# A ratio moved eight steps behind the sums it is made from, and a unit's sums, inverse, scaling and turn moved one to three steps later

## The chip, the core and the metric

The kernel runs on one core of a Trainium2 chip. A core has a matrix engine (PE in the profile, with its weight loads as PEld), a vector engine (DVE, called VectorE below), a scalar engine (ACT, ScalarE), a general engine (POOL, GpSimd), and SyncE (SP), which issues most of the DMAs. Each engine works through its own list of instructions in order; an instruction whose input is not there yet holds up everything behind it on that engine. The metric is the device time of one execution in microseconds; less is better.

## The reference: what is computed

A transformer block on 2048 rows of 1024 numbers, all in 32-bit floats.

```python
qkv = (layernorm(x) @ wqkv)            # 32 heads of 32
pq, pk = q @ w_phi[h], k @ w_phi[h]    # per head
phi_q = concat(softmax(pq), softmax(-pq))   # 64 features; phi_k alike
kv = phi_k^T v ; z = sum over rows of phi_k
o  = (phi_q kv) / (phi_q z + 1e-6)
h  = x + o @ wo
out = h + relu(layernorm(h) @ w1) @ w2      # w1: 1024 x 3584, w2: 3584 x 1024
```

The part that the change touches is phi_q and the division. For a row and a head let e+ = exp(pq - max), e- = exp(min - pq), and s+, s- their sums. The kernel does not divide e+ and e- by their sums one by one. It forms the **ratios of the two signs' sums**, s+/s- and s-/s+, because up to a common factor, which the division by the denominator takes out, one ratio is all that a sign's features need.

## The kernel before

**Matmuls and their weights.** Every large matmul is made of three passes (lines 182 to 184): each operand is a rounded high part and a remainder, and high x high, high x low and low x high are added. A weight tile comes from memory into a `raw` buffer (six of them), ScalarE rounds it (line 125), VectorE or GpSimd subtracts to get the low part (line 129), and PE uses both from a ring of ten `w` tiles. The tile is free again when the last matmul that needs it is done.

**Items and steps.** The work on PE is a list of items. An item is one 128 x 512 result; it has eight steps, and a step is one weight tile, so three matmuls. Everything else is hung beside this list: `when(step, f, ...)` issues function f right after that step's matmuls have been written. That order of writing is the order of each engine's list. It gives no time: an engine may run behind, or ahead as far as its inputs allow.

**The stretch in question.** It goes from the last items for the queries to the output projection. Let step 0 be `8 * (last_kv + 4)`. The query items run up to step 104; there the output projection (`wo`) begins, four items of pairs of row tiles (first those tiles' products with `wo` columns 0 to 511), then single items, to step 360.

For each query item (its first step is 8n):

- after its last matmul: VectorE's `q_first`, four passes over the result in PSUM (lines 516, 517, 520, 521: maximum, minimum, two differences);
- step 8n + 14, `q_second`: ScalarE's exponential (line 525) and the store of it to a scratch tensor `ed`;
- step 8n + 19, `q_third`: VectorE's sums (`qsm`, line 533) and their inverse (line 534), and **at once behind it GpSimd's two products for the ratio** (`smq`, line 536), which need that inverse;
- after a group of four row tiles: SyncE stores the ratios (`sm_store`, line 540, step 8n + 30) and loads them again turned (`sm_load` into `smx`, line 544, step 8n + 44, for the last group 8n + 72).

The attention itself is done in 32 **units** u (one unit: 512 rows, four heads, both signs). Unit u begins at step s(u) = 19u/2 for u under 8, and 16 + 8u from u = 8 on. Its steps before the change, counted from s(u):

| step | function | engine, line | what |
|---|---|---|---|
| -5 | at_load | SP, 544 | loads the exponentials, four DMAs |
| 6, 9 | at_sums | POOL, 588 | product with z, a half each (`ez`) |
| 8, 11 | at_reduce | DVE, 595 | sums over 32 features, a half each (`qtz`) |
| 13 | at_cross | ACT, 606 | brings the other sign's sums across |
| 16 | at_den | POOL, 610, 611 | denominators, with the ratio |
| 17 | at_inverse | DVE, 614 | their inverse |
| 19 | at_scale | POOL, 619 / 624 | scales the exponentials |
| 23 | at_turn | DVE, 630 | turns 32 x 32 blocks |
| 30 (odd u) | at_num | PE, 643 | numerators of units u - 1 and u, then ScalarE's line 650 |
| 32 (odd u) | at_low | DVE, 660 | low part of the attention's output `oT` |

For u under 6 the steps from at_sums to the inverse were done earlier, so only load, scaling (line 619) and turn stand here, and at_num and at_low come 6 steps later. So numerators stand at steps 45, 64, 83 (u = 1, 3, 5), 96 (u = 7), 118, 134, 150 and every 16 steps from there on.

Beside the output projection also run: VectorE's addition of an item's result (`wo_add`, lines 697 and 700), and the second layernorm on pairs of tiles, i = 0 to 3 (`ln_pair`): load (line 216), 9 steps later VectorE's statistics (line 222), then GpSimd (231 to 233), ScalarE (239) and transposes on PE (246). The statistics of i = 0 to 3 stand at steps 177, 217, 257 and 297.

Of the kernel before, what the change touches and what calls it, by code (L numbers as in the profile page):

```python
# [140 lines left out]
def kernel(  # L141
# [47 lines left out]
    def do(n, k, f, *args):  # L189
        at[n, k].append((f, args))  # L190
# [5 lines left out]
    place_of = {t: (b, i) for b, tiles in enumerate(groups) for i, t in enumerate(tiles)}  # L196
# [333 lines left out]
    def q_third(s, t):  # L530
        b, i = place_of[t]
        sm = zk.tile([P, 2, 2, 16], F32, name="qsm", bufs=2)
        v.tensor_reduce(out=sm[:, 0].rearrange("p s (a c) -> p a s c", a=4), in_=e_of.pop((s, t)), op=ALU.add, axis=AX.X)  # L533
        v.reciprocal(sm[:, 1], sm[:, 0])
        for k in range(2):
            pool.tensor_tensor(out=smq[:, b % 2, i, k, 16 * s:16 * (s + 1)], in0=sm[:, 0, k], in1=sm[:, 1, 1 - k],
                               op=ALU.mult)
# [402 lines left out]
    def item(gen, *args, keys):  # L940
        items.append((gen, args + (keys,)))
        steps.extend((k,) for k in keys)
        return len(items) - 1
# [11 lines left out]
    for b, tiles in enumerate(groups):  # L955
        for hf in range(2):

            pairs = b == 0 and hf == 0
            for j in range(0, 4, 2 if pairs else 1):
# [3 lines left out]
                for half in range(2):  # L963
                    n = item(wo_pair, tiles[j:j + 2], hf, half, keys=[("wo", hf, 4 * half + k // 2) for k in range(8)])
# [26 lines left out]
    def when(step, f, *args):  # L991

        if step < 8 * first_up:
            do(step // 8, step % 8, f, *args)
        else:
            do(first_up + (step - 8 * first_up) // 4, step % 4, f, *args)
# [4 lines left out]
    for t in range(1, NT):  # L1001
        n = t - 1 if t < HT else q_n[1, t - HT] + 1
# [106 lines left out]
    for (sl, t), n in q_n.items():  # L1109
        when(8 * n + 14, q_second, sl, t)  # L1110
        when(8 * n + 19, q_third, sl, t)
        b, i = place_of[t]
        if (sl, i) == (1, 3):
            when(8 * n + 30, sm_store, b)
            when(8 * n + (44, 44, 44, 72)[b], sm_load, b)
    for u in range(32):
        start = 8 * (a0 + u) if u >= 8 else 8 * (last_kv + 4) + 19 * u // 2
        slack = 6 if u < 6 else 0

        for step, f, *args in ((-5, at_load), (6, at_sums, 0), (8, at_reduce, 0), (9, at_sums, 1), (11, at_reduce, 1),  # L1120
                               (13, at_cross), (16, at_den), (17, at_inverse), (19, at_scale), (23, at_turn)):
            if u >= EARLY or f in (at_load, at_scale, at_turn):
                when(max(start + step, 8 * (last_kv + 4)), f, u, *args)
        if u % 2:
            when(start + 30 + slack, at_num, u)
            when(start + 32 + slack, at_low, u)
        if u < EARLY:
            start = 8 * (kv_n[1, u // 2, NT - 1] + 4) + (-2, 19)[u % 2]
            for step, f in ((0, early_load), (9, early_sums), (14, early_reduce), (17, at_cross), (20, at_den), (22, early_scale)):
                when(start + step, f, u)  # L1130
# [35 lines left out]
    def up_step(b, p, m):  # L1166

        return up0 + 4 * (up_n[b, p, m] + 1 - first_up)

    for j, m in enumerate(UP):  # L1170

        for g in range(2):
            step = up0 + (8 * j + (-62, -29)[g] if j < 4 else 6 * (j - 4) + 4 + 2 * g)
# [4 lines left out]
            step = up_step(0, NP - 1, m) + 2 * j  # L1178
# [4 lines left out]
    for b in range(2):  # L1183
        for p in range(NP):
            for m, k, f, *args in UP_BESIDE:
                if f is up_store:
                    args = [b, p, *args]
# [7 lines left out]
    for n, (w, p, j) in enumerate((w, p, j) for w in (1, 2) for p in range(NP) for j in range(2)):  # L1195
        step = sums_at[n]
# [7 lines left out]
    for b in range(2):  # L1204
        for m in DOWN:
            n = down_n[b, m, NP - 1] + 1
# [110 lines left out]
```

## Time and profile before

| | us |
|---|---|
| median of three runs | 1881.74 |
| lowest, highest run | 1880.16, 1882.63 |
| profiled execution, its own time | 1884.99 |
| its span in the trace | 1883.2 |
| PE busy (99% of the span) | 1863.4 |
| VectorE, ScalarE, GpSimd busy | 1067.7, 771.2, 979.0 |

The profiled execution is 3.25 us above the median of the runs, and 1.8 us of its time lie outside the span. PE is busy in nearly all of it, so the busy share as such says little: what another engine can cost or save is the little time in which PE waits, and the time in which it works at a lower clock. In the rows of a timeline the first number is the start from the span's beginning, the second the duration; a wait stands in brackets, with the instruction that ended it. "x2" after a row counts instructions merged into it, and a merged row's time is theirs together.

### The profile page before, as it was taken

Reading aid. Unit: us, or ns where it says so; the run is one execution under the profiler, and the core shown is the slowest. Engines: PE = TensorE matmul, PEld = TensorE weight load, DVE = VectorE, ACT = ScalarE, POOL = GpSimd, SP = SyncE. Lnnn points to the kernel's source line nnn. Section 1 sums busy time; section 2 is a strip of 40 time slices with the busy share of each in tenths; the row PEclk is TensorE's granted clock in tenths of the full one; section 3 lists DMA queues with packets and bytes.
Section 4 is the critical chain, followed back from the end, with each engine's and each line's share of the span. In section 5 each row is a group of like instructions: output and inputs, shape, how many; then the busy total and the mean of one; then the engine's idle time right before and its main releaser. Section 6 shows DMA issues by size and latency. Waiting matters only on the chain.

```text
span 1883.2 us, 29093 instructions
## 1 busy us (share of the span) xinstructions
PE 1863.4 (99%) x10064; PEld 1520.1 (81%) x10064; DVE 1067.7 (57%) x1655; ACT 771.2 (41%) x1379; POOL 979.0 (52%) x991
## 2 busy tenths in 40 slices
PE   9999999999999899999999999999999999999999
PEld 7777788888886677888888888888888888888887
DVE  6788678677679877565555563444433433343333
ACT  5322244233333334355455554444444444444442
POOL 3887744888946988443233222222344444444443
PEclk9999999999999999999999999999999999999999
DMA  6888787666675898797889985666676677767775
GB/s 212 291 291 293 232 292 255 209 197 201 177 206 170 213 234 207 256 290 213 260 257 261 316 279 177 190 192 215 207 240 217 206 225 238 239 214 217 217 215 177
DMA packets 348963, 433.05 MB, mean 230 GB/s; under 512 B 32272, under 2 KB 219664, under 8 KB 348816
## 3 DMA queue, kind: packets, MB, share of 16 engines
q1 hardware_dynamic: 331920, 414.42, 72.5%
q10 hardware_dynamic: 16896, 16.78, 2.7%
q8 instruction: 79, 1.29, 0.3%
q14 instruction: 68, 0.56, 0.1%
HBM read 293.21 MB, written 137.89 MB: 229 GB/s over the span
## 4 chain that ended last, share of the span: by engine, by line
PE 93%; DVE 2%; POOL 1%; issue 1%; DMA 1%; ACT 1%; SPq 0%; ACTq 0%; DVEq 0%; POOLq 0%
PE mm L182 24%; PE mm L183 24%; PE mm L184 24%; PE ac L182 4%; PE ac L184 4%; PE ac L183 4%; PE tp L182 2%; PE tp L184 2%; PE tp L183 2%; PE tp L246 1%; PE ac L465 1%; PE ac L643 1%; POOL w L129 0%; DVE qsm L533 0%; DVE qe L630 0%
## 5 line engine op out<-in xcount | busy, mean ns | idle before, releaser
L129 POOL TENSOR_TENSOR w<-raw,w 128x512 fp32r<-128x512 f32 x353 | 469.1, 1331 | 681.3 <-ACT w L125 659.3
L125 ACT ACTIVATE w<-raw 128x512 fp32r<-128x512 f32 x686 | 409.5, 626 | 509.4 <-PE mm L184 238.0
L129 DVE TENSOR_TENSOR w<-raw,w 128x512 fp32r<-128x512 f32 x333 | 272.9, 820 | 512.1 <-ACT w L125 501.0
L182 PE MATMUL mm<-w,xT 128*128 128x512 f32 x768 | 305.9, 398 | 0.0
L183 PE MATMUL mm<-w,xT 128*128 128x512 f32 x768 | 300.5, 391 | 0.3 <-POOL w L401 0.3
L184 PE MATMUL mm<-w,xT 128*128 128x512 f32 x768 | 300.0, 391 | 0.0
L183 PE MATMUL mm<-hT,w 128*128 128x512 f32 x672 | 261.4, 389 | 0.0
L182 PE MATMUL mm<-hT,w 128*128 128x512 f32 x672 | 261.4, 389 | 0.0
L184 PE MATMUL mm<-hT,w 128*128 128x512 f32 x672 | 261.4, 389 | 0.0
L182 PEld LDWEIGHTS mm<-w,xT 128*128 128x128 f32 x768 | 144.6, 188 | 35.0 <-issue 3.7
L184 PEld LDWEIGHTS mm<-w,xT 128*128 128x128 f32 x768 | 144.5, 188 | 30.9
L183 PEld LDWEIGHTS mm<-w,xT 128*128 128x128 f32 x768 | 144.7, 188 | 29.3 <-POOL w L401 0.9
L363 POOL TENSOR_TENSOR b<-b 128x256 f32<-128x256 f32 x176 | 144.0, 819 | 35.6 <-DMA b<-in_w_dram 26.0
L182 PE MATMUL mm<-w 128*128 128x512 f32 x392 | 152.5, 389 | 0.0
L183 PE MATMUL mm<-w 128*128 128x512 f32 x392 | 152.5, 389 | 0.0
L184 PE MATMUL mm<-w 128*128 128x512 f32 x392 | 152.5, 389 | 0.0
L183 PEld LDWEIGHTS mm<-hT,w 128*128 128x128 f32 x672 | 126.1, 188 | 26.4
L182 PEld LDWEIGHTS mm<-hT,w 128*128 128x128 f32 x672 | 126.1, 188 | 26.2
L184 PEld LDWEIGHTS mm<-hT,w 128*128 128x128 f32 x672 | 126.1, 188 | 26.1
L184 PEld LDWEIGHTS mm<-w 128*128 128x128 f32 x392 | 73.6, 188 | 15.3
L182 PEld LDWEIGHTS mm<-w 128*128 128x128 f32 x392 | 73.6, 188 | 15.3
L183 PEld LDWEIGHTS mm<-w 128*128 128x128 f32 x392 | 73.6, 188 | 15.3
(173 smaller groups left out, 3116.8 us busy)
## 6 DMA issues: line engine op xcount, KB each, us to landing
raw<-t SPq DMA_DIRECT2D x224, 256.0 KB, 3.8
raw<-ad SPq DMA_DIRECT2D x196, 256.0 KB, 3.0
raw<-in_w_dram SPq DMA_DIRECT2D x168, 256.0 KB, 3.1
ad<-c SPq DMA_DIRECT2D x112, 256.0 KB, 3.6
b<-in_w_dram SPq DMA_DIRECT2D x44, 512.0 KB, 6.0
t<-b SPq DMA_DIRECT2D x44, 512.0 KB, 5.1
ad<-s SPq DMA_DIRECT2D x84, 256.0 KB, 4.1
ed<-qe ACTq DMA_DIRECT2D x32, 512.0 KB, 4.4
```

The costliest lines, as they stand in the source:

```text
L125: nc.scalar.activation(w[:, 0, :], raw[1], AF.Copy)
L129: eng.tensor_tensor(out=w[:, 1, :], in0=raw[1], in1=w[:, 0, :].bitcast(F32), op=ALU.subtract)
L182: pe.matmul(ps, a_hi, b_hi, start=first, stop=False, skip_group_check=more)
L183: pe.matmul(ps, a_hi, b_lo, start=False, stop=False, skip_group_check=more)
L184: pe.matmul(ps, a_lo, b_hi, start=False, stop=last, skip_group_check=more)
L246: pe.transpose(pt[:, k, :], xn[:, (4 * j + k) * P:(4 * j + k + 1) * P], ident)
L363: pool.tensor_tensor(out=tsum[*u, *out], in0=tsum[*u, *a], in1=tsum[*u, *b], op=ALU.subtract)
L465: pe.matmul(kv_ps[s][g][32 * i:32 * (i + 1), 0:64], vt[:, 32 * h:32 * (h + 1)], phi[:, 64 * h:64 * (h + 1)], start=first, stop=last)
L643: pe.matmul(banks[g][32 * c:32 * (c + 1), 256 * j:256 * (j + 1)], kvL[rows, 2 * q + h // 4, 32 * (h % 4):32 * (h % 4 + 1)], phT_of[u - 1 + ...
```

## The change

Two tables of steps are changed, and one function is cut in two.

- `q_third` keeps VectorE's sums and inverse at step 8n + 19. The two products on GpSimd become `q_fourth`, at step 8n + 27. Since a step's functions are written in the order of the items, the ratio of one item now stands just ahead of the sums of the next.
- The ratios' store goes from 8n + 30 to 8n + 34, and their load from 8n + 44 to 8n + 48; the last group's load stays at 8n + 72.
- In the units, the reductions go from 8 and 11 to 10 and 12, cross from 13 to 14, the inverse from 17 to 18, scaling from 19 to 20, and the turn from 23 to 26. The loads, products, denominators and numerators stay.

No instruction is added or taken away, and no tile or buffer count is changed.

```diff
@@ q_third
         v.reciprocal(sm[:, 1], sm[:, 0])
+        sm_of[s, t] = sm
+
+    sm_of = {}
+
+    def q_fourth(s, t):
+        b, i = place_of[t]
+        sm = sm_of.pop((s, t))
         for k in range(2):
             pool.tensor_tensor(out=smq[:, b % 2, i, k, 16 * s:16 * (s + 1)], in0=sm[:, 0, k], in1=sm[:, 1, 1 - k],
                                op=ALU.mult)
@@ the table of steps
         when(8 * n + 14, q_second, sl, t)
         when(8 * n + 19, q_third, sl, t)
+        when(8 * n + 27, q_fourth, sl, t)
         b, i = place_of[t]
         if (sl, i) == (1, 3):
-            when(8 * n + 30, sm_store, b)
-            when(8 * n + (44, 44, 44, 72)[b], sm_load, b)
+            when(8 * n + 34, sm_store, b)
+            when(8 * n + (48, 48, 48, 72)[b], sm_load, b)
...
-        for step, f, *args in ((-5, at_load), (6, at_sums, 0), (8, at_reduce, 0), (9, at_sums, 1), (11, at_reduce, 1),
-                               (13, at_cross), (16, at_den), (17, at_inverse), (19, at_scale), (23, at_turn)):
+        for step, f, *args in ((-5, at_load), (6, at_sums, 0), (10, at_reduce, 0), (9, at_sums, 1), (12, at_reduce, 1),
+                               (14, at_cross), (16, at_den), (18, at_inverse), (20, at_scale), (26, at_turn)):
```

What this does to the engines' lists is shown at three places. From line 536 on, a line's number in the changed kernel is 7 higher than before (line 619 is 626 there, 630 is 637). The numbers behind the names tell one buffer's use from another's; they differ a little between the two kernels.

**First place: GpSimd's list where the first units are scaled** (units 0, 1 and 2; `smq<-qsm` is a ratio, `qe<-qe,smx` a scaling, `w<-raw,w` the low part of a query weight). Before:

```order
L536 TENSOR_TENSOR smq_2999<-qsm_6231 128x16 x2
L619 TENSOR_TENSOR qe_6131<-qe_6131,smx_3000 128x1024
L536 TENSOR_TENSOR smq_2999<-qsm_6276 128x16 x2
L619 TENSOR_TENSOR qe_6153<-qe_6153,smx_3000 128x1024
L129 TENSOR_TENSOR w_6307<-raw_5880,w_6307 128x512
L129 TENSOR_TENSOR w_6320<-raw_5891,w_6320 128x512
L129 TENSOR_TENSOR w_6328<-raw_5904,w_6328 128x512
L536 TENSOR_TENSOR smq_2999<-qsm_6336 128x16 x2
```

And now:

```order
L626 TENSOR_TENSOR qe_6129<-qe_6129,smx_3000 128x1024
L543 TENSOR_TENSOR smq_2999<-qsm_6231 128x16 x2
L626 TENSOR_TENSOR qe_6151<-qe_6151,smx_3000 128x1024
L129 TENSOR_TENSOR w_6304<-raw_5880,w_6304 128x512
L129 TENSOR_TENSOR w_6317<-raw_5891,w_6317 128x512
L129 TENSOR_TENSOR w_6325<-raw_5904,w_6325 128x512
L543 TENSOR_TENSOR smq_2999<-qsm_6276 128x16 x2
```

Each ratio has moved behind the scaling that it stood ahead of: the second scaling now stands behind the ratio of `qsm_6231`, where it stood behind that of `qsm_6276`, which is made one item later.

**Second place: VectorE's list around the turn of unit 7**, the last one ahead of the output projection (`qe_6525`, now `qe_6522`). Before:

```order
L520 TENSOR_TENSOR qe_6746<-mm_6677,qmx_6743 128x4x128
L521 TENSOR_TENSOR qe_6746<-qmx_6743,mm_6677 128x4x128
L595 TENSOR_REDUCE qtz_6753<-ez_6738 128x16
L630 STREAM_TRANSPOSE qe_6525<-qe_6525 128x1024
L533 TENSOR_REDUCE qsm_6767<-qe_6674 128x4x2x4
L534 RECIPROCAL qsm_6767<-qsm_6767 128x32
L595 TENSOR_REDUCE qtz_6753<-ez_6759 128x16
```

And now:

```order
L520 TENSOR_TENSOR qe_6744<-mm_6670,qmx_6741 128x4x128
L521 TENSOR_TENSOR qe_6744<-qmx_6741,mm_6670 128x4x128
L602 TENSOR_REDUCE qtz_6759<-ez_6736 128x16
L533 TENSOR_REDUCE qsm_6766<-qe_6667 128x4x2x4
L534 RECIPROCAL qsm_6766<-qsm_6766 128x32
L637 STREAM_TRANSPOSE qe_6522<-qe_6522 128x1024
L602 TENSOR_REDUCE qtz_6759<-ez_6754 128x16
```

The turn has moved behind one more query item's sums and inverse.

**Third place: VectorE's list around the statistics of pair i = 2** of the second layernorm, beside the turn of unit 27 (`qe_8008`, now `qe_8006`). Before:

```order
L630 STREAM_TRANSPOSE qe_8008<-qe_8008 128x1024
L595 TENSOR_REDUCE qtz_8289<-ez_8276 128x16
L614 RECIPROCAL qden_8268<-qden_8268 128x32
L700 TENSOR_TENSOR xh_8173<-mm_8223,xh_8171 128x4x4x32
L758 BN_STATS hst_8298<-xh_8173 128x6
L222 BN_STATS st_8300<-xin_8233 128x6 x2
L224 BN_AGGR mv_8303<-st_8300 128x2
L222 BN_STATS st_8305<-xin_8235 128x6 x2
```

And now:

```order
L707 TENSOR_TENSOR xh_8171<-mm_8222,xh_8169 128x4x4x32
L765 BN_STATS hst_8294<-xh_8171 128x6
L222 BN_STATS st_8296<-xin_8230 128x6 x2
L224 BN_AGGR mv_8299<-st_8296 128x2
L222 BN_STATS st_8301<-xin_8232 128x6 x2
L224 BN_AGGR mv_8304<-st_8301 128x2
L637 STREAM_TRANSPOSE qe_8006<-qe_8006 128x1024
L621 RECIPROCAL qden_8271<-qden_8271 128x32
```

The turn has moved from ahead of the addition to behind the addition and the statistics.

## Prediction

> **What bounds the kernel now.** I read the page first, then PE's busy time by stretches, then the timelines of PE and of the engines it waits for.
>
> ```profile
> span 1883.2 us, 29093 instructions
> ...
> PE 1863.4 (99%) x10064; PEld 1520.1 (81%) x10064; DVE 1067.7 (57%) x1655; ACT 771.2 (41%) x1379; POOL 979.0 (52%) x991
> ```
>
> PE is busy for 99%: 19.8 us of the span are idle, so no change beside PE can win more than these and what a lowered clock costs. The next view cuts the stretch in question at the starts of numerators (u = 3, 5, 7, 9, 11, 13, 15).
>
> ```profile
> core 0: us, PE busy (x) PEld busy (x) DVE busy (x) ACT busy (x) POOL busy (x), PEclk, DMA share, GB/s
> 566.73:580.90 14.17, 14.17 (x91) 11.11 (x90) 14.10 (x23) 4.87 (x9) 6.95 (x10) 1.00 0.69 207
> 580.90:590.98 10.08, 10.08 (x72) 7.79 (x71) 8.25 (x14) 3.37 (x8) 4.98 (x9) 1.00 0.62 175
> 590.98:618.74 27.76, 19.91 (x100) 13.99 (x99) 26.25 (x36) 11.23 (x25) 20.80 (x24) 0.91 0.56 153
> 618.74:631.68 12.94, 12.94 (x82) 9.60 (x81) 10.74 (x15) 4.73 (x14) 12.11 (x14) 0.93 0.92 219
> 631.68:647.60 15.92, 13.96 (x89) 10.27 (x95) 14.79 (x19) 4.57 (x14) 15.69 (x16) 0.89 0.79 186
> 647.60:659.73 12.13, 12.13 (x89) 9.42 (x95) 8.80 (x14) 3.50 (x13) 11.59 (x12) 1.00 1.00 235
> ```
>
> By the table of steps these rows hold 19, 13, 22, 16, 16 and 16 steps and one pair of numerators each. The first and the last are undisturbed (clock 1.00, PE busy throughout): 14.17 - 12.13 over three steps gives 0.68 us a step, and so 1.25 for the numerators. The second (13 steps, 10.09) fits. The third should then take 16.21, the fourth and fifth 12.13. They take 27.76, 12.94 and 15.92: **11.55 + 0.81 + 3.79 = 16.15 us** are lost here. VectorE is busy for 26.25 of the 27.76 and GpSimd for 15.69 of the 15.92.
>
> PE's timeline shows where (start, duration, engine, line, names and shapes, the wait ahead in brackets):
>
> ```profile
> 590.98 0.97 PE L643 MATMUL ac<-qe,kvL 64*32 64x256 f32 x16
> 595.50 0.76 PE L643 MATMUL ac<-qe,kvL 64*32 64x256 f32 x16 [3.54 <-POOL ez L588]
> ...
> 612.89 0.50 PE L183 MATMUL mm<-w,oT 128*128 128x512 f32 x1 [1.26 <-POOL w L129]
> ...
> 617.58 0.80 PE L183 MATMUL mm<-w,oT 128*128 128x512 f32 x1 [3.05 <-DVE w L129]
> ...
> 634.30 1.20 PE L643 MATMUL ac<-qe,kvL 64*32 64x256 f32 x16 [1.96 <-DVE qe L630]
> ```
>
> The waits of the stretch are 3.54 (numerators of unit 7), 1.26 and 3.05 (low parts of two `wo` tiles) and 1.96 (numerators of unit 11), 9.8 together. The other 6.3 of the 16.15 are slow matmuls: the granted clock is 0.91, 0.93 and 0.89 in those rows. Behind the 1.26 the next matmul takes 0.50 us, behind 3.05 it takes 0.80, so I give the short wait no clock loss. The last row's 3.79 - 1.96 = 1.9 then belong to the wait of 1.96, and the rest, 3.7 + 0.8, I split evenly by their lengths: 2.3 behind 3.54, 2.1 behind 3.05.
>
> Here a rule can be weighed. The Trainium skill (TensorE: Matmul & The Clock Gate, "What's actually happening") says that the array falls to half clock after at least one idle window of about 3.4 us. The trace disagrees, since 1.96 us was enough. By the rule that wait would have cost nothing more, and the sum below would save 1.9 us less.
>
> Why is VectorE late? Because of one wait:
>
> ```profile
> 543.86 0.40 POOL L536 TENSOR_TENSOR smq<-qsm 128x16 f32<-128x16 f32 x2 [5.23 <-DVE qsm L534]
> 544.22 1.92 POOL L619 TENSOR_TENSOR qe<-qe,smx 128x1024 f32<-128x1024 f32 x1
> 546.10 3.81 POOL L129 TENSOR_TENSOR w<-raw,w 128x512 fp32r<-128x512 f32 x3
> ...
> 550.22 3.78 POOL L129 TENSOR_TENSOR w<-raw,w 128x512 fp32r<-128x512 f32 x3
> 553.95 1.93 POOL L619 TENSOR_TENSOR qe<-qe,smx 128x1024 f32<-128x1024 f32 x1
> ```
>
> ```profile
> 543.89 4.04 ACT L125 ACTIVATE w<-raw 128x512 fp32r<-128x512 f32 x6 [0.52 <-PE mm L184]
> ```
>
> ```profile
> 550.56 0.68 DVE L521 TENSOR_TENSOR qe<-qmx,mm 128x512 f32<-128x512 f32 x1
> 555.91 1.25 DVE L630 STREAM_TRANSPOSE qe<-qe 128x1024 f32<-128x1024 f32 x1 [4.68 <-POOL qe L619]
> ...
> 584.20 0.69 DVE L595 TENSOR_REDUCE qtz<-ez 128x16 f32<-128x512 f32 x1 [1.76 <-POOL ez L588]
> ...
> 591.18 0.68 DVE L516 TENSOR_REDUCE qmx<-mm 128x16 f32<-128x512 f32 x1
> ...
> 594.17 1.23 DVE L630 STREAM_TRANSPOSE qe<-qe 128x1024 f32<-128x1024 f32 x1
> ...
> 615.10 2.43 DVE L129 TENSOR_TENSOR w<-raw,w 128x512 fp32r<-128x512 f32 x1
> ```
>
> GpSimd stood 5.23 us for an inverse at 543.86; behind it were the scaling of unit 1, six weight tiles that ScalarE had begun to deliver at 543.89, and the scaling of unit 2 (553.95). VectorE waited 4.68 us for that one with the turn. The wait of 3.54 is put down to GpSimd, but what came last was turn 7: 594.17 + 1.23 = 595.40, and PE goes on at 595.50. From 555.91 on VectorE never catches up: the query item whose first pass is at 591.18 had ended on PE at about 584.7 (590.98 less the step of the next item and the item, 0.68 and 5.5), 6.5 us earlier.
>
> **The change part by part.**
>
> *The ratio behind the next item's sums.* GpSimd's wait of 5.23 goes: the ratio it now meets there is one whose sums were ready an item earlier. The six tiles then start when ScalarE's first is ready, 543.89 + 0.65 = 544.5, take six times 1.25 and one ratio pair of 0.40, and end at 552.4; the scaling of unit 2 (1.93) ends at 554.3, not 555.9. So this gives only 1.6 of the 4.68 by itself. But VectorE no longer stands idle up to then, since the turn also moved:
>
> ```profile
> L533 DVE TENSOR_REDUCE qsm<-qe 128x32 f32<-128x1024 f32 x32 | 38.4, 1201 | 0.0
> L630 DVE STREAM_TRANSPOSE qe<-qe 128x1024 f32<-128x1024 f32 x32 | 39.6, 1236 | 19.2 <-POOL qe L624 12.0 <-POOL qe L619 7.1
> ```
>
> *The turn three steps later.* A pair of sums and inverse (1.2 + 0.3 = 1.5) now runs ahead of turn 2, in the time of the old wait. VectorE's next work starts 1.6 + 1.5 = 3.1 us earlier. The same inverse that GpSimd waited for also caused the 1.76 at 584.20; it goes as well. Together 4.9; I take 4.4 at 591.18, since the first half's sums of unit 6 will still wait a little for their product.
>
> *Unit 7.* VectorE begins that item's four passes (2.4) at 586.8, then half sums (0.6), then, new, 1.5 of sums and inverse, then the turn (1.2): it ends at 592.5. PE wants it half a numerator pair after 590.98, at 591.5. The wait falls from 3.54 to 1.0, and a wait of 1.0 costs no clock. Saved: 2.5 + 2.3 = 4.8. The bounds: 5.9 if it vanishes, 2.0 if VectorE gains only the 1.6.
>
> *The `wo` tile on VectorE* (615.10, PE's 617.58). PE comes 4.8 earlier. VectorE comes 4.4 earlier, but its tile now stands behind the turn of unit 8, and the tile ahead of it behind ScalarE's cross of unit 9. So the two waits 1.26 + 3.05 = 4.3 stay in sum at 4.3 to 5.1; I take 4.7, with the same 2.1 of clock. Lost: 0.4. Bounds: nothing left (saved 6.4), or 2 us more.
>
> *Units 11 and 13.* Summed along VectorE's list from the `wo` tile on, turn 11 comes about 0.4 after PE's want, not 1.96, and the clock loss of 1.9 goes. Then GpSimd is the limit (busy for 12.11 of 12.94 and 15.69 of 15.92):
>
> ```profile
> 643.03 1.92 POOL L624 TENSOR_TENSOR qe<-qe,qden 128x1024 f32<-128x1024 f32 x1
> ```
>
> This is the scaling of unit 13. PE is 4.8 - 0.4 + 1.96 + 1.9 - 0.4 = 7.9 earlier by then and wants the turn at 647.60 + 0.55 - 7.9 = 640.25. GpSimd's lead I put at 5.2, between VectorE's 4.4 at unit 7 and the 5.9 by which turn 11 comes earlier: the scaling ends at 639.75, the turn at 640.95, a wait of 0.7. Saved on both: 1.96 + 1.9 - 0.4 - 0.7 = 2.8. Bounds: 0 and 3.9.
>
> Sum of the stretch: 4.8 - 0.4 + 2.8 = **7.2 of the 16.15**.
>
> *From unit 15 on* both engines run level with PE. A unit's turn now follows the addition that PE's item end releases (0.6 + 1.2), and its numerators come six steps (4.1 us) and half a pair behind that end: cover 2.9 us. Cross now stands behind ScalarE's copies of the numerators, which waits for PE; what hides it is the period that a scaling has until its turn (6 us). Cost taken: 0. One place lacks the cover, the statistics of i = 2, ahead of which the turn of unit 27 stood:
>
> ```profile
> 731.50 3.31 SPq L216 DMA_DIRECT2D xin<-hd  x2
> ```
>
> ```profile
> 718.15 1.77 DVE L738 TENSOR_TENSOR xin<-xin,s 128x512 f32<-128x512 f32 x1
> ...
> 723.59 0.63 DVE L700 TENSOR_TENSOR xh<-mm,xh 128x512 f32<-128x512 f32 x1
> ...
> 736.57 1.29 DVE L222 BATCH_NORM_STATS2 st<-xin 128x6 f32<-128x512 f32 x2 [1.30 <-DMA xin<-hd]
> 740.29 1.29 DVE L222 BATCH_NORM_STATS2 st<-xin 128x6 f32<-128x512 f32 x2 [2.19 <-DMA xin<-hd]
> ```
>
> ```profile
> 735.99 1.09 PE L643 MATMUL ac<-qe,kvL 64*32 64x256 f32 x32
> ```
>
> ```profile
> PE tp L246 <- ACT xin L239: 1.7, 1, 1.7
> ...
> PE tp L246 <- ACT xin L248: 0.8, 1, 0.8
> ```
>
> Here the loads of `xin` come late (1.30 and 2.19), and turn 27 would begin at 741.7 and end at 742.9 where PE wants its half of the numerators of 735.99 at 736.5: 6.4 us. But on SyncE's queue the loads (731.50) come behind one that waits for the addition at 723.59, and this addition no longer stands behind an inverse that waited for GpSimd; it follows line 738 (718.15 + 1.77) and one half sum, at 720.5. So the loads come 3.1 earlier: a wait of 3.3, with 2.3 of clock, 5.6. Against it go the waits of 1.7 and 0.8 for the same pair's normalisation (PE now comes later than it), with an estimated 0.8 of slow matmuls, 3.3. Net **loss 2.3**; bounds 0 and 5.4. The statistics of i = 0 stand so by unit 17, but without a late load: 0 to 0.3, taken as 0.
>
> *SyncE's queue.* The ratios' store moves behind one `wo` load (row tiles 8 to 11), their load behind another; unit 16's denominators stand 48 steps (33 us) behind that load. Nothing.
>
> Sum: -7.2 + 2.3 = **-4.9 us**. The profiled execution would have 1884.99 - 4.9 = 1880.1 and a span of 1878.3; the median of the runs lies 3.25 below the profiled time, so I predict 1881.74 - 4.9 = **1876.8 us**.
>
> **The rivals.**
>
> - *VectorE catches up altogether* (0.17). The `wo` tile's wait goes too, 4.7 and 2.1 more: -11.7, 1870.0. For it: 4.4 us of lead against a wait of 3.05. Against it: PE gains the same lead, and ScalarE's list is not freed.
> - *Unit 27 at its full price* (0.11). If the loads of i = 2 are not earlier, 6.4 + 2.3 - 3.3 = 5.4 are lost: -1.8, 1879.9, which can't be told from no change (0.2%, or 3.8 us, is about the least that this measurement can tell).
> - *GpSimd's new work slows VectorE's splits* (0.05):
>
> ```profile
> 562.09 0.71 DVE L129 TENSOR_TENSOR w<-raw,w 128x512 fp32r<-128x512 f32 x1
> ```
>
>   The same subtraction takes 0.71 here and 2.43 at 615.10, where GpSimd is at work throughout. Five splits of the stretch, each slower by up to 0.7, cost VectorE 3.7 (5 x 0.74): -1.2, 1880.5. Beside it stands the Trainium skill (GPSIMD Engine Reference, "1. Specifications"): GpSimd shares its SBUF interfaces with VectorE, with contention for VectorE's instructions with two SBUF inputs. The trace agrees.
> - *The later turns cost more than they free* (0.18): slower. Turns are written four steps ahead of the numerators, no longer seven. If VectorE is over 2.9 us behind an item's end when it comes to a turn, PE waits for what stands ahead of it. GpSimd's six tiles keep the lead at 3.1, the turns of units 7, 11 and 13 each pay 1.5, and unit 27 pays 5.4: -3.1 + 4.5 + 5.4 = +6.8, 1888.5. For it: VectorE was 6.5 behind. Against it: at unit 11 the additions, not the turn, fill the time.
> - *Nothing moves* (0.04): GpSimd waits elsewhere, 1881.7.
>
> **How the numbers follow.** The forecast has 0.45, within 1873 to 1880 by the bounds of its terms; three quarters of that lie under 1878.0. Faster: 0.45 x 0.75 + 0.17 + 0.02 from the second = 0.53. Same: 0.45 x 0.25 + 0.09 + 0.05 + 0.04 = 0.29, of which 0.02 go to the slower side for terms that I took at nothing. Slower: 0.18 + 0.02 = 0.20. The range goes from the first rival's time, which leaves out half of it, to 1887, which leaves out most of the slower one: 1870.0 to 1887.
>
> **What would show it.** Right: no wait of GpSimd for the inverse of 5 us near 540; VectorE's turn 2 about 1.6 earlier; the numerators of unit 7 waiting about 1; the `wo` wait still there; PE waiting 3 us at unit 27's numerators, and none at the transposes behind them. Wrong: a wait for the turn at most odd units, or none at all at the `wo` tile.

## The result: no difference that can be measured

The changed kernel takes 1881.78 us (median of 20 runs, 1877.44 to 1884.93), the kernel before 1882.92 (20 runs, 1879.48 to 1884.57); the ratio is 0.9995, interval 0.9989 to 1.0002. Forecast were 1876.8 us and a gain of 4.9; the measured gain is 1.1, not told apart from none. The profiled execution of the changed kernel took 1877.44, the least of its 20, so its trace shows the change at its best. From its page, and from the view of waits for PE's rows:

```profile
span 1875.6 us, 29094 instructions
...
PE 1859.8 (99%) x10064; PEld 1517.2 (81%) x10064; DVE 1070.5 (57%) x1655; ACT 771.3 (41%) x1379; POOL 981.3 (52%) x991
```

```profile
PE ac L650 <- DVE qe L637: 4.0, 4, 1.7
PE mm L183 <- DVE w L129: 1.8, 1, 1.8
...
PE tp L246 <- ACT xin L248: 1.5, 1, 1.5
PE ac L650 <- POOL ez L595: 1.3, 1, 1.3
...
PE mm L183 <- POOL w L129: 0.4, 1, 0.4
```

The long waits of before (3.54, 3.05, 1.96) have given way to many of 0.4 to 1.8 us. The stretch of the prediction, cut again at the starts of the numerators of units 3, 5, 7, 9, 11, 13 and 15:

```profile
core 0: us, PE busy (x) PEld busy (x) DVE busy (x) ACT busy (x) POOL busy (x), PEclk, DMA share, GB/s
564.72:578.88 14.16, 14.16 (x90) 11.10 (x89) 14.06 (x24) 4.17 (x9) 9.23 (x12) 1.00 0.92 223
578.88:588.97 10.09, 10.09 (x72) 7.73 (x72) 10.05 (x16) 4.08 (x8) 6.51 (x11) 1.00 0.39 119
588.97:609.58 20.61, 17.14 (x100) 12.65 (x99) 18.84 (x29) 8.36 (x19) 16.53 (x19) 1.00 0.70 206
609.58:624.06 14.48, 14.07 (x82) 10.29 (x81) 12.04 (x16) 6.43 (x19) 12.61 (x16) 0.88 0.90 220
624.06:637.65 13.59, 12.45 (x81) 9.39 (x81) 10.99 (x16) 4.66 (x14) 13.43 (x13) 1.00 0.72 185
637.65:650.96 13.31, 12.50 (x82) 9.40 (x81) 10.36 (x16) 2.92 (x11) 13.08 (x16) 1.00 1.06 251
```

The third row took 27.76 us before and takes 20.61. The last three take 14.48, 13.59 and 13.31 where 12.13 is undisturbed: the loss is now spread over all of them.

At the first place that the prediction spoke of, GpSimd's and VectorE's timelines of the changed kernel read:

```profile
542.58 3.82 POOL L129 TENSOR_TENSOR w<-raw,w 128x512 fp32r<-128x512 f32 x3 [5.96 <-ACT w L125]
546.36 0.40 POOL L543 TENSOR_TENSOR smq<-qsm 128x16 f32<-128x16 f32 x2
546.72 3.78 POOL L129 TENSOR_TENSOR w<-raw,w 128x512 fp32r<-128x512 f32 x3
550.47 1.91 POOL L626 TENSOR_TENSOR qe<-qe,smx 128x1024 f32<-128x1024 f32 x1
```

```profile
552.40 1.25 DVE L637 STREAM_TRANSPOSE qe<-qe 128x1024 f32<-128x1024 f32 x1 [1.82 <-DMA ed<-qe]
...
588.09 1.21 DVE L533 TENSOR_REDUCE qsm<-qe 128x32 f32<-128x1024 f32 x1
589.34 0.35 DVE L534 RECIPROCAL qsm<-qsm 128x32 f32<-128x32 f32 x1
589.61 1.19 DVE L637 STREAM_TRANSPOSE qe<-qe 128x1024 f32<-128x1024 f32 x1
```

GpSimd's wait for the inverse ahead of the six tiles is gone; it now waits there for ScalarE's rounding, as forecast. The turn's 1.82 us of waiting are put down to a DMA in this row, but GpSimd's scaling ends at 552.38, and the turn begins at 552.40. All times here are 2.0 us lower than in the profile before, since PE reaches the numerators of unit 1 at 550.55 and not at 552.56. That is not the change: in the profile before the clock stood at half once more from 9.53 to 12.95 us, which no other profile shows between its first 8 us and unit 1, and in no other does PE come to unit 1 later than 551.2.

### Five profiles of the two kernels

Since one execution proved a poor witness, both kernels were profiled again (in the first two experiments below and in the last). The distances between the starts of numerators, in us:

| execution | unit 1 to 15 | 15 to 25 | 25 to 29 | sum |
|---|---|---|---|---|
| before, first | 107.10 | 64.20 | 29.06 | 200.4 |
| before, second | 108.19 | 64.21 | 27.38 | 199.8 |
| changed, first | 100.41 | 66.32 | 28.07 | 194.8 |
| changed, second | 100.36 | 66.32 | 30.84 | 197.5 |
| changed, third | 101.98 | 66.70 | 32.26 | 200.9 |
| least seen in any kernel | 100.4 | 64.2 | 26.1 | |

In the mean the changed kernel is 6.7 us faster up to unit 15, and loses 2.2 between units 15 and 25 and 2.2 between 25 and 29. From unit 29 to 31 each of the five takes 12.13 us, and from there to the end of the span 1118.1, so all that the change does lies in this table.

### The profile page after: what moved, and what is told of

The parts are those of the page before. It is cut to its first block, busy times and chain, and to the rows that moved or that the text cites. A ratio compares the mean times of both kernels' runs of the same rounds, so it can differ in the third digit from the quotient of the medians.

```text
span 1875.6 us, 29094 instructions
## 1 busy us (share of the span) xinstructions
PE 1859.8 (99%) x10064; PEld 1517.2 (81%) x10064; DVE 1070.5 (57%) x1655; ACT 771.3 (41%) x1379; POOL 981.3 (52%) x991
## 3 DMA queue, kind: packets, MB, share of 16 engines
q8 instruction: 79, 1.29, 0.3%
## 4 chain that ended last, share of the span: by engine, by line
PE 92%; DMA 2%; DVE 2%; POOL 2%; issue 1%; ACT 0%; SPq 0%; DVEq 0%; POOLq 0%; ACTq 0%
PE mm L182 24%; PE mm L183 23%; PE mm L184 23%; PE ac L182 4%; PE ac L184 4%; PE ac L183 4%; PE tp L182 2%; PE tp L184 2%; PE tp L183 2%; PE tp L246 1%; PE ac L465 1%; DMA qe<-ed 1%; POOL qe L631 1%; DMA ed<-qe 1%; POOL ez L595 0%
## 5 line engine op out<-in xcount | busy, mean ns | idle before, releaser
L182 PEld LDWEIGHTS mm<-hT,w 128*128 128x128 f32 x672 | 126.1, 188 | 26.1
```

Of the source, the lines that this page charges most:

```text
L182: pe.matmul(ps, a_hi, b_hi, start=first, stop=False, skip_group_check=more)
```

## Experiments

### The two kernels again, and each half of the change alone

**The kernel before, unchanged.**

> The kernel before, unchanged: a second execution under the profiler. Theory A (waits are a property of the order): the same waits of PE within 0.3 us each: 3.54 at unit 7, 1.26 and 3.05 at the wo tiles, 1.96 at unit 11, 1.7 and 0.8 in the second layernorm. Theory B (what a wait costs in clock is decided anew in each execution): the same waits, but the matmuls at half clock behind a part of them only, and not behind the same ones; the stretch from unit 1 to unit 15 then takes anything from 101 (no loss) to 107 us. Theory C (the waits vary, with the DMAs): waits that differ by over 1 us. Time 1882.9, as in the runs so far (1879.5 to 1884.6).

1882.35 us (11 runs), ratio to the kernel before 0.9996, interval 0.9987 to 1.0004. PE waits 3.55, 1.25 and 3.04 as in the first profile (3.54, 1.26, 3.05), but 3.08 at unit 11 where the first has 1.96, and 0.78 in the second layernorm where it has 1.73 + 0.78. So A holds for the first three, and the stretch, 108.19, lies a little above the range given. B holds too: the matmuls behind the wait of 3.04 run at full clock this time, and PE came to unit 11 that much earlier, and waited longer for a turn that VectorE finished at its own time. So the wait that differs by over 1 us, which was C's sign, follows here from B; no DMA is needed for it.

**The changed kernel, unchanged.**

> The changed kernel, unchanged: a second execution under the profiler; the first was the fastest of its 20 runs (1877.44, granted clock 0.999, median 1881.78). Theory A: the waits are again 1.3 at unit 7, 1.8 at the wo tile, 1.1 at unit 11, 0.8 at unit 13, 1.7 at unit 27 and 1.5 at the transposes of the second layernorm, 10 us in all. Theory B: these same waits, but with half clock behind two to four of them, at about 2 us each, so that unit 1 to unit 15 takes 102 to 105 us where it took 100.4. Theory C: waits longer by over 1 us where the first profile had short ones. Time 1881.8.

1881.85 us (11 runs), ratio 0.9998, 0.9989 to 1.0006. Up to unit 15 nothing differs by over 0.1 us. At unit 27 the wait is 2.85, and the clock is at half from 734.26 to 737.67; a third execution is shown last. C holds there, and only there. Half clock follows two of the waits, this one and, as in the first profile, that at 609; unit 1 to 15 takes 100.36, under the range that B gave.

**The ratio alone** (the unit's steps as before):

```diff
-        for step, f, *args in ((-5, at_load), (6, at_sums, 0), (10, at_reduce, 0), (9, at_sums, 1), (12, at_reduce, 1),
-                               (14, at_cross), (16, at_den), (18, at_inverse), (20, at_scale), (26, at_turn)):
+        for step, f, *args in ((-5, at_load), (6, at_sums, 0), (8, at_reduce, 0), (9, at_sums, 1), (11, at_reduce, 1),
+                               (13, at_cross), (16, at_den), (17, at_inverse), (19, at_scale), (23, at_turn)):
```

> Only the ratio moved behind the next item's sums; the unit's steps as before. By the prediction's terms GpSimd's wait of 5.2 us goes, its scaling of unit 2 ends 1.6 earlier, VectorE gains 1.6 there and 1.8 at the place where it waited for the next product: unit 7's wait falls from 3.5 to 0.5 to 1.9, that of the wo tiles stays at 4 to 5 in sum, unit 27's turn is not moved and PE doesn't wait for it: 3 to 5 us faster than before, 1878 to 1880. The rival, that the ratio alone frees nothing because the six weight tiles behind it hold GpSimd up as long: unit 7's wait 3 to 3.5, time 1882.9 as before.

**1879.49 us**, ratio 0.9985, 0.9977 to 0.9994: 2.9 us faster than before, by itself more than the whole change. From PE's timeline:

```profile
591.76 0.76 PE L650 MATMUL ac<-qe,kvL 64*32 64x256 f32 x16 [2.10 <-POOL smq L543]
...
628.76 0.76 PE L650 MATMUL ac<-qe,kvL 64*32 64x256 f32 x16 [3.08 <-DVE qe L637]
```

Unit 7 waits 2.10, a little more than expected; the `wo` tiles wait 1.27 and 1.27, less than expected; PE doesn't wait at unit 27, and the stretch from 15 to 25 is undisturbed at 64.21.

**The unit's steps alone** (the ratio at once behind its sums, the new table of steps).

> Only the unit's steps moved; the ratio stays at once behind its sums. GpSimd still waits about 5 us for the inverse near 540, and VectorE still comes to the end of unit 2's scaling at about 555.9, but with 1.5 us of sums and inverse already done. Theory of the prediction: the turn of unit 7 then stands behind one more pair of sums and inverse: the lead of 1.5 is given back there, unit 7's wait 3 to 4, and unit 27 waits 2 to 3 us where it did not: 1 to 4 us slower than before, 1884 to 1887. The rival (the later turn alone is what brings the gain, since VectorE fills its wait with sums): unit 7's wait under 2, time 1879 to 1881.

1881.87 us, ratio 0.9999, 0.9990 to 1.0008: neither the loss nor the gain. This kernel is made from the one before and has its line numbers. From PE's timeline:

```profile
592.03 1.15 PE L643 MATMUL ac<-qe,kvL 64*32 64x256 f32 x16 [2.38 <-POOL smq L536]
...
612.72 1.20 PE L643 MATMUL ac<-qe,kvL 64*32 64x256 f32 x16 [2.08 <-DVE qe L630]
...
734.01 0.76 PE L643 MATMUL ac<-qe,kvL 64*32 64x256 f32 x16 [3.04 <-DVE qe L630]
```

Both theories missed the early part. The new steps shorten unit 7's wait without the ratio's move (2.38, not 3 to 4): VectorE no longer stands 2.39 us at a turn ahead of the passes of the next item, so the inverse that GpSimd waits for comes 1.0 us sooner (GpSimd goes on at 540.92 behind a wait of 4.29; in the second profile of the kernel before at 541.92 behind 5.24). GpSimd's six tiles start at 543.16, only 0.6 later than with both, and VectorE does a pair of sums in the time ahead of the turn. Unit 1 to 15 takes 101.93, almost as with both. The late part is as expected: 3.04 at unit 27, which the kernel with the ratio alone doesn't have. So **the new steps gain early and lose late**.

### Where the late loss comes from

The chain ahead of the second pair's transposes (i = 1), from the timelines of VectorE, GpSimd, ScalarE and PE in the first profile of the changed kernel:

```profile
695.61 1.29 DVE L222 BATCH_NORM_STATS2 st<-xin 128x6 f32<-128x512 f32 x2 [1.36 <-DMA xin<-hd]
...
698.18 0.31 DVE L621 RECIPROCAL qden<-qden 128x32 f32<-128x32 f32 x1
...
698.64 1.92 POOL L631 TENSOR_TENSOR qe<-qe,qden 128x1024 f32<-128x1024 f32 x1 [4.23 <-DVE qden L621]
...
707.07 0.94 ACT L613 ACTIVATE qden<-qtz 32x32 f32<-32x32 f32 x4 [1.61 <-DVE qtz L602]
708.04 1.09 ACT L248 ACTIVATE xin<-tp 128x512 f32<-128x512 f32 x2
...
708.69 0.66 PE L246 MATMUL tp<-ident,xin 128*128 128x128 f32 x4 [1.51 <-ACT xin L248]
```

At step 217 stand the statistics of i = 1. The change moved the turn of unit 22 from 215 to 218 and the inverse of unit 23 from 217 to 218, so both now stand behind them, and the statistics wait for a load. GpSimd stands 4.23 us for that inverse, its later products come late, so do the half sums and ScalarE's cross, and behind cross stand the copies that PE's transposes need. In the same way units 17 and 18 were moved across the statistics of i = 0, and 27 and 28 across those of i = 2. Three experiments put parts of this back.

**The turn of unit 27 alone:**

```diff
-                               (14, at_cross), (16, at_den), (18, at_inverse), (20, at_scale), (26, at_turn)):
+                               (14, at_cross), (16, at_den), (18, at_inverse), (20, at_scale), (23 if u == 27 else 26, at_turn)):
```

> The changed kernel with one thing put back: the turn of unit 27 at step 23, ahead of the statistics of pair i = 2; every other list is the same. If the wait of PE at unit 27's numerators (1.67 in one execution, 2.85 with one stretch at half clock in the other) comes from standing behind the statistics, it is gone, and the waits at the transposes of that pair come back (0.8 to 2.5): 1 to 3.5 us faster than the changed kernel, 1878.5 to 1881. The rival, that the late load of the statistics only moves the wait on to the transposes at its full length: no change, 1881.8.

1878.99 us, ratio 0.9982, 0.9974 to 0.9991. By the medians (1881.85 and 1878.99, from two comparisons in which the kernel before took 1882.41 and 1882.33) one instruction is worth 2.9 us. Its profile doesn't show that gain: PE no longer waits at unit 27, but

```profile
739.70 1.10 PE L246 MATMUL tp<-ident,xin 128*128 128x128 f32 x8 [1.03 <-ACT xin L239]
...
745.15 0.66 PE L246 MATMUL tp<-ident,xin 128*128 128x128 f32 x4 [2.28 <-ACT xin L248]
```

so that units 25 to 29 took 29.86, and in that execution the rival was right: the wait had moved on to the transposes. The profiled execution spans 1878.5, which is above what the median of its runs would have; the loss at this place changes with the loads from one execution to the next.

**All six instructions back ahead of the statistics:**

```diff
-                               (14, at_cross), (16, at_den), (18, at_inverse), (20, at_scale), (26, at_turn)):
+                               (14, at_cross), (16, at_den), (17 if u in (18, 23, 28) else 18, at_inverse), (20, at_scale),
+                               (23 if u in (17, 22, 27) else 26, at_turn)):
```

> The changed kernel with the instructions put back that had moved from ahead of to behind the statistics of pairs i = 0, 1 and 2: the turns of units 17, 22 and 27 at step 23, the inverses of units 18, 23 and 28 at step 17. If all of the late loss comes from these, PE's wait of 1.5 at the second pair's transposes goes too (there GpSimd stood 4.3 us for the inverse of unit 23): another 1.5 to 2.1 us less than with the turn of unit 27 alone, 1876.5 to 1879. The rival, that the wait at these transposes comes from ScalarE's cross, which stays where it is: the same as with turn 27 alone.

**1875.11 us**, ratio 0.9956, 0.9942 to 0.9970; measured again:

> The kernel with the six instructions put back ahead of the statistics, measured again beside the other two: 1875.1 as in its five runs so far (1873.3 to 1875.7), 7 us faster than before.

**1874.30 us**, ratio 0.9964, 0.9952 to 0.9977. That is 7 us less than before and than the changed kernel, better than expected. Units 15 to 25 take 64.21 in both profiles, units 25 to 29 take 26.69 and 26.07. The only late wait in the first one's timeline of PE:

```profile
740.37 0.66 PE L246 MATMUL tp<-ident,xin 128*128 128x128 f32 x4 [0.37 <-ACT xin L248]
```

The late loss of the change comes from these six instructions, and so the rival, that cross by itself makes the transposes wait, falls: cross stands where the change put it.

**The new steps only up to unit 15:**

```diff
+        old = u > 15
+        for step, f, *args in ((-5, at_load), (6, at_sums, 0), (8 if old else 10, at_reduce, 0), (9, at_sums, 1),
+                               (11 if old else 12, at_reduce, 1), (13 if old else 14, at_cross), (16, at_den),
+                               (17 if old else 18, at_inverse), (19 if old else 20, at_scale), (23 if old else 26, at_turn)):
```

> The ratio moved, the new steps for units 0 to 15 alone, the old steps from unit 16 on. If the new steps gain in the stretch up to unit 15 (100.4 us from unit 1 to unit 15, where the ratio alone takes 103.7 and the kernel before 107 to 108) and lose behind it (unit 15 to 31: 106.5 and 109.3, where the ratio alone takes 104.6), both halves add up: 100.4 + 104.6 = 205, against 212 before: 5 to 7 us faster than before, 1875.5 to 1877.5. The rival, that PE's earlier arrival meets the same late loads and the gain turns into longer waits at the second layernorm: 1879 to 1880, like the ratio alone.

1877.33 us, ratio 0.9971, 0.9960 to 0.9983: both halves add up, as expected. It is 2 to 3 us above the kernel with the six put back, since the old late steps keep waits of 0.98 and 0.77 at the third pair's transposes, and one of 0.82 stands at unit 15's numerators, where the two tables meet.

### What a wait costs in clock

The granted clock, read in slices of 0.1 us, around the slow matmuls at 611 us of the changed kernel (start and end, length, PE's busy time and instructions, clock, DMA share, GB/s):

```profile
610.60:610.80 0.20, 0.14 (x8) 1.00 1.41 231
610.80:610.90 0.10, 0.10 (x8) 0.69 1.06 169
610.90:611.00 0.10, 0.10 (x12) 0.50 1.37 236
...
614.10:614.20 0.10, 0.10 (x2) 0.50 0.73 287
614.20:614.30 0.10, 0.10 (x2) 0.74 1.00 389
614.30:614.50 0.20, 0.20 (x2) 1.00 0.97 327
```

The clock is 0.5 from 610.84 to 614.25, 3.41 us. Twelve of the thirteen profiles have such places between the numerators of unit 1 and those of unit 31 or just behind them: 29 in all, each 3.41 or 6.83 us long, and within a profile they lie whole multiples of 3.41 us apart. If a grid of that pitch is laid out from the slow places, each of the 29 follows a window in which PE's waits fill 0.48 to 0.96 of the time. Of the 76 other windows with a wait in them, at full clock, none has over 0.51; in the thirteenth profile, which has no such place, none has over 0.45. So this place follows from the wait of 1.76 that ends at 608.91, all but its first 0.28, and the one of 0.41 that ends at 610.65: they share a window and fill 1.89 us of it. To try this on purpose, waits were made:

```diff
         v.transpose(ph, ph)
+        if u % 2 and u >= 15:
+            for k in range(8):
+                v.transpose(ph[:, 0:512], ph[:, 0:512])
```

> The ratio moved, the old steps, and behind the turn of each odd unit from 15 to 31 eight further turns of half of its tile, which leave it as it was: about 5 us more on VectorE, of which some 2.8 are covered, so nine waits of PE of 2 to 2.5 us each. Theory W, from the traces so far: the clock is halved for a fixed window of 3.41 us where PE stood idle for more than half of the window before, and these windows run on whatever the kernel does: 5 to 7 of the nine waits are followed by a slow window, at 1.7 us each, at places that follow from the idle share of each window: 25 to 33 us slower than the ratio alone in all. The rule by length that the prediction used (about 2 us of lost clock behind each wait of 2 us): all nine, 36 to 40 us. If only a whole idle window counts: none, 18 to 22 us.

1920.11 us, 40.6 above the ratio alone. From PE's timeline, three of the nine:

```profile
673.81 0.77 PE L653 MATMUL ac<-qe,kvL 64*32 64x256 f32 x16 [0.46 <-issue]
...
710.56 1.21 PE L653 MATMUL ac<-qe,kvL 64*32 64x256 f32 x16 [5.07 <-issue]
...
761.41 0.76 PE L653 MATMUL ac<-qe,kvL 64*32 64x256 f32 x16 [1.77 <-issue]
```

The waits are not as even as meant: 0.46 to 5.07, 23.7 in sum. Each of the eight of 1.77 and more is followed by half clock, three of them for two windows; the one of 0.46 is followed by none: 11 windows at up to 1.7 make 18.8, of which the waits that reach into these windows take back some. The time alone would fit the rule by length, and theory W's range was too low for waits of this size; but the windows are W's, all of one length and on one grid. That only a whole idle window counts is excluded: six of the eight are shorter than a window.

### Unit 11, and the changed kernel a third time

**Unit 11 earlier as well** (added to the six; the beginning of the first line of each is left out):

```diff
-... (17 if u in (18, 23, 28) else 18, at_inverse), (20, at_scale),
-                               (23 if u in (17, 22, 27) else 26, at_turn)):
+... (17 if u in (11, 18, 23, 28) else 18, at_inverse),
+                               (17 if u == 11 else 20, at_scale),
+                               (20 if u == 11 else 23 if u in (17, 22, 27) else 26, at_turn)):
```

> The kernel with the six instructions put back ahead of the statistics, and unit 11 made earlier as well: its inverse and scaling at step 17, its turn at step 20, so that GpSimd scales it ahead of one product of unit 12 and VectorE turns it ahead of one half sum and one weight split that took 2.14 us. PE's wait at unit 11's numerators (2.76, with 6.83 us of half clock behind it) should fall to 0.3 to 0.8 and lose no clock: 2 to 4 us faster than without, 1871 to 1873. The rival, that unit 12's product or the weight tile is then late in its place: a new wait of 1 to 2 at unit 13 or at the weights, no gain.

1874.42 us, ratio 0.9965, 0.9951 to 0.9978; without it 1874.30. Unit 11 waits 0.68, no slow window is left, but

```profile
631.22 0.50 PE L183 MATMUL mm<-wf,oT 128*128 128x512 f32 x1 [0.78 <-POOL wf L129]
...
639.75 0.76 PE L650 MATMUL ac<-qe,kvL 64*32 64x256 f32 x16 [1.75 <-DVE qe L637]
```

By the medians the rival was right: GpSimd has no room there (13.43 of 13.59 us busy in the changed kernel, in the table above), and what unit 11 is spared comes back as waits at a weight tile and at unit 13. The profiles alone would say otherwise, since units 1 to 15 take 100.40 with it, and 102.23 and 102.17 without; but the profiled executions without it lie 0.5 and 1.1 us above the medians of their runs, and that with it 0.4 below.

**The changed kernel, third time.**

> The changed kernel, a third execution under the profiler. The waits up to unit 15 again 1.3, 0.4, 1.8, 0.4, 1.1, 0.8; at unit 27, where it hangs on a late load, 1.5 to 3. Time 1881.8; 6 to 7 us above the kernel with the six instructions put back.

1881.32 us, ratio 0.9999, 0.9990 to 1.0007, and 7 above the kernel with the six put back, as expected. Unit 11, however, waited 2.74, not 1.1: without a slow window at 611 PE comes sooner to a turn that ends at 625.8. PE's numerators of unit 27 in the three profiles of the changed kernel, first, second and third:

```profile
731.74 0.76 PE L650 MATMUL ac<-qe,kvL 64*32 64x256 f32 x16 [1.67 <-DVE qe L637]
```

```profile
733.17 0.76 PE L650 MATMUL ac<-qe,kvL 64*32 64x256 f32 x16 [2.85 <-DVE qe L637]
```

```profile
735.24 1.20 PE L650 MATMUL ac<-qe,kvL 64*32 64x256 f32 x16 [3.21 <-DVE qe L637]
```

and on VectorE in the third, behind a load that ends late:

```profile
732.55 1.29 DVE L222 BATCH_NORM_STATS2 st<-xin 128x6 f32<-128x512 f32 x2 [1.47 <-DMA xin<-hd]
...
734.00 1.19 DVE L637 STREAM_TRANSPOSE qe<-qe 128x1024 f32<-128x1024 f32 x1
```

## Why the prediction held, and where it did not

The time lies within the range that was given, 1870.0 to 1887, but this range holds no change as well as the forecast, so that proves little. The forecast, 4.9 us faster, did not come; of the rivals none describes the result as a whole.

- **The ratio moved: right.** Less the 2.0 us by which this trace starts ahead, GpSimd's scaling of unit 2 and VectorE's turn of it come 1.5 us earlier (550.47 for 553.95, 552.40 for 555.91); 1.6 was forecast.
- **Unit 7: right.** The turn ends at 590.80, and PE waits 1.26, where 1.0 was forecast, with no clock lost.
- **The `wo` tile: wrong in size.** Forecast were 4.7 us of waits and 2.1 of clock; there are 0.45 + 1.76, and 0.41 at unit 9, with one slow window in two of three executions. The split that I took at 2.43 us takes 0.63 in its new place (last section). Here the first rival, a VectorE that catches up, was nearer than the forecast.
- **Units 11 and 13: wrong the other way.** Forecast were waits of 0.4 and 0.7; there are 1.14 and 0.81 if a slow window came ahead, and 2.74 with two slow windows if none did. VectorE isn't the reason: its turn of unit 11 ended at 634.25 before and ends at 625.80 now, 6.4 us earlier less the 2.0, where 5.9 was forecast. PE is: it wants this turn 5.6 us earlier than before in the first profile and 7.2 in the third, where 4.4 was forecast, since it lost less at the `wo` tiles. On VectorE before and now, and on PE now:

```profile
633.02 1.23 DVE L630 STREAM_TRANSPOSE qe<-qe 128x1024 f32<-128x1024 f32 x1
```

```profile
624.57 1.23 DVE L637 STREAM_TRANSPOSE qe<-qe 128x1024 f32<-128x1024 f32 x1
```

```profile
625.86 0.76 PE L650 MATMUL ac<-qe,kvL 64*32 64x256 f32 x16 [1.14 <-DVE qe L637]
```

- **The stretch in sum: right**, -6.7 for -7.2. The two errors have one cause: what PE does not lose at the `wo` tiles it waits at unit 11, for a turn whose time was forecast to 0.5 us.
- **Unit 27: right in kind, and by luck in size.** Forecast were a wait of 3.3, with the clock 5.6 in all, against 3.3 recovered at the transposes; measured are waits of 1.67, 2.85 and 3.21, and losses of 2.0, 4.8 and 6.2, in the mean 4.3, against the undisturbed 26.07. The kernel before lost 3.0 and 1.3 here, in the mean 2.2. Both terms were over 1 us too large, and so the net is +2.2, for +2.3.
- **"From unit 15 on ... Cost taken: 0" is the step that failed**, with its sentence that only one place lacks the cover. I followed the turns and looked for late loads at i = 0 and i = 2. At i = 1 an inverse, too, had been moved across the statistics, and GpSimd waits for it: 2.1, 2.1 and 2.5 us that were not in the sum.
- **The clock terms** (2.3, 2.1 and 1.9 us behind three waits) were each one window of 3.41 us at half clock, 1.7. What I had split by the waits' lengths is a step, taken or not. Three windows make 5.1 of the 6.3 us that I put down to the clock; the other 1.2 lie outside them, and what they are stays open.

Of the signs of being wrong, a wait for the turn at most odd units, a part is there: in the first profile units 7, 9, 11, 13 and 27 wait for it, the other odd units don't.

In sum the profiles give -6.7 + 2.2 + 2.2 = -2.3. The medians of the three comparisons give -1.1, -0.6 and -0.2, with intervals that reach from about -2 to +1. In the mean that is 1.7 less gain than the profiles give. Most of this is chance: the three profiled executions of the changed kernel (1877.44, 1880.48 and 1883.60) lie in the mean 1.1 below the medians of their runs. What the rest is stays open.

The mechanism of the forecast is borne out by the kernel with the six instructions put back: the stretch's gain without the late loss, 7 us.

## What to carry to other kernels

When steps are moved in a table, list for every engine which instructions change places with one that waits for a DMA, not only those of the step that seems to matter: here three turns and three inverses had crossed three groups of statistics, and putting these six back was worth 7 us, as much as the change gains in its early stretch. If a change gains in one stage and loses in another, keep it where it gains; each half should be tried by itself. For effects under half a per cent, compare the same stretch in several executions: one profile was the best of 20 runs, the other carried 2 us from a place far from the change.

## What the runs showed of the hardware that I had not expected

**The clock gate counts in fixed windows.** Windows of 3.41 us run on through an execution, and about half a window of waiting is enough to halve the clock for the next one: the least share that was followed by half clock was 0.48, the largest that was not 0.51. Two short waits in one window do it (1.48 and 0.41 us ahead of 610.84), and none of the four waits of 1.47 to 1.52 that had no other in their windows did. So a wait that is alone in its window cost no clock below about 1.6 us (0.48 of 3.41), and beyond that it depends on how it falls on the grid, which differs from run to run: the same wait of 3.05 was followed by half clock in one execution of the kernel before and not in the other. When the clock comes back is less clear: after a slow window with no wait in it, or with 0.04 of it, it always did; after those with waits of 0.11 to 0.14 of their length in two of four cases, and from 0.18 on in none of six. Beside this stands the Trainium skill (TensorE: Matmul & The Clock Gate, "What's actually happening"), which gives a free-running window of 3413 ns; the traces agree with that to the hundredth. It ties half clock to an idle window; here about half an idle window was enough. The prediction weighed that rule as if it needed a wait of 3.4 us.

**VectorE's subtraction and GpSimd's work exclude each other, one instruction at a time.** From VectorE's and GpSimd's timelines of the changed kernel:

```profile
597.17 2.35 DVE L129 TENSOR_TENSOR w<-raw,w 128x512 fp32r<-128x512 f32 x1
...
608.23 0.63 DVE L129 TENSOR_TENSOR w<-raw,w 128x512 fp32r<-128x512 f32 x1
```

```profile
597.06 1.91 POOL L631 TENSOR_TENSOR qe<-qe,qden 128x1024 f32<-128x1024 f32 x1
...
608.21 1.79 POOL L595 TENSOR_TENSOR ez<-qe,zb 128x512 f32<-128x512 f32 x1
```

The first split meets a scaling that ends at 598.97 and itself ends at 599.52, 0.55 us later: it stood until GpSimd was done. In this profile 65 splits begin while a GpSimd instruction that began earlier has over 0.2 us to run; 64 of them end 0.54 to 0.55 us behind it, and where no GpSimd instruction overlaps a split it takes 0.67 to 0.70. The one exception is the second row: at 608.2 the two begin within 0.02 us of each other, VectorE takes 0.63, and GpSimd's product, 1.29 when nothing holds it up, takes 1.79, so here VectorE went first. So the 2.43 of the profile before was 0.63 and a wait, and its price depends on what GpSimd happens to be doing, not on how busy it is. The Trainium skill (SBUF — State Buffer, "SBUF: two separate sides") states an exclusive lock for the whole instruction on the shared ports; the trace agrees.
